# Two blocks of the second product in seven quarter products, with a new order table

## The chip, the cores and the metric

The kernel runs on one NeuronCore of one Trainium2 chip. The metric is the device time of one execution in microseconds; the figure before the change is the median of three runs. All times of single instructions come from one further, profiled execution.

## What is computed

Windowed attention with global tokens (8 batches, 8 heads, 512 local and 32 global tokens, head size 64) feeds a two-layer block with the gate h·cos(h). The second layer's product, `g @ w_out`, is what the change touches.

```python
s_ll = np.where(np.abs(pos[:, None] - pos[None, :]) <= 32, scale * q_l @ k_l.T, -1e9)
out_l = sm(concat([scale * q_l @ k_g.T, s_ll])) @ concat([v_g, v_l])
out_g = sm(scale * q_g @ concat([k_g, k_l]).T) @ concat([v_g, v_l])
x = concat([out_g, out_l])        # 8*544 tokens x 512
h = x @ w_in                      # w_in 512 x 2048
g = h * np.cos(h)
return g @ w_out                  # w_out 2048 x 512
```

## The kernel before

All matrix operands are kept as pairs of 16-bit floats, a high and a low part. A product of two such pairs is three matmuls: high by high, high by low, low by high.

**The chunks.** The tokens of the second stage are cut into 17 chunks of 256: chunks 0 to 15 hold the local tokens (two per batch, so chunk c belongs to batch c // 2), chunk 16 (`NC`) all 256 global ones. The 2048 columns of `w_in` are cut into 8 blocks of 256 (`NS`, index j), each of two tiles of 128.

**The first product** of a block is `m1_a(c, j)` (L1369): 2 tiles x 4 slices of the inner dimension x 3 = 24 matmuls with 256 moving columns, each with its own weight load, into one PSUM bank `ph` (three of these rotate). The gate follows: `m1_b` (ScalarE L1386, VectorE L1387) makes the argument `u`, `m1_c` the sine (ScalarE L715), `m1_d` the gated value `gf` (VectorE L1404), its high part `gh` (ScalarE L1408) and its low part `gl` (GpSimd L1409). Eleven places (`NG`) hold `gh` and `gl`; three hold `u`.

**The second product** of a block is `m2_a(c, j)` (L1423 to L1425): the moving operand is a row tile of `w_out` with 512 columns, the weights are 128x128 pieces of `gh` or `gl`. 2 token halves k x 2 tiles x 3 = 12 matmuls of 512 columns go into `po[0]` and `po[1]`, two PSUM banks of 128x512, where all 8 blocks of a chunk are summed. `m2_b` scales `po[0]` out of PSUM on ScalarE (L1438) and `po[1]` on VectorE (L1436); the very last bank is split between both (L1432, L1433). `m2_c` writes it out (L1445, L1453).

**Around it** attention of batches 2 to 7 is spread over chunks 2 to 13: scores (L1125, L1126), minimum and exponent (VectorE L1142, ScalarE L715), normalizing and splitting (GpSimd L1171, L1178, ScalarE L1176), transposes by DMA (L1183) and the product with the values (L1215). Sine and exponent share line 715 and need different tables on ScalarE; each change of kind is an ACT_TABLE_LOAD.

**What sets the order.** The program emits its work in numbered steps (one call such as `m1_a(4, 2)` is one step). `ORDER` holds a string for each engine and one for the DMA queue of SyncE: `599x24` means the next 24 instructions of step 599 on that engine, `23.4` means instruction 4 of step 23. Consecutive entries are tied, so every engine runs exactly in the order of its string and waits in that order.

Of the kernel before, what the change touches and what calls it, by code (L numbers as in the profile page):

```python
# [22 lines left out]
        18x4 22x4 23.4 23.0 23.5 23.1x2 23.6 23.3 23.7 27x4 29.4x4 29.0x2 33 33.2 33.1 33.3 29x2 28x8  # L23
        34x8 35 35.4 35.1x3 35.5x2 40.4 49 35 40.0x2 40.5 40.2 40.6x2 40.3 57 39x8 69x4 41x8 74 74.2
        74.1 74.3 108 108.2 64x24 67x24 72x24 91x24 108.1 108.3 106x24 125x24 109 109.4 109.1 109.5
        109.2 109.6 109.3 109.7 135x7 110x2 110.4 110.2x2 110.5x3 135 143x6 112x8 113x4 124 127x4 141x8
        113x4 143x2 135x16 149x3 149.4 149.3 149.5x3 143x16 150 150.4 150.1 150.5 150.2 150.6 150.3
        150.7 151x8 155 155.4 155.1x3 152x8 156x20 157x8 164x8 189x5 189.6x5 189.5 189.11 164x16 170x5
        176x24 208 208.6x2 208.1x2 208.8x2 208.3x2 171x20 195x4 187x24 208 208.10x2 196 196.2 196.1
        196.3 206x19 227x24 229.6 206x5 229 229.0x3 229.8 229.3x2 229.9x3 229.5 250.6x2 250.0x2 250.8x3  # L30
        250.2x4 250.11 204 209x4 274x4 274.6x3 274.4 274.9x2 274.5 274.11 210x2 210.3 210.2 288.6x3
        288.0x6 288.9x3 300x4 300.6x4 300.4 300.10x2 300.5 230 231x8 233 233.2 233.1 233.3 248x24 272x24
        234 234.2 234.1 234.3 303.6 303.0x3 303.7x3 303.3x3 303.10x2 230x35 311x12 251 252x4 313x4 313.6
        313.4 313.7x5 313.5 253x4 251x35 318x5 318.6x2 318.5 318.8x4 325x3 325.6x6 325.3x3 275x12 276x8
        286x24 275x24 349x5 329x2 329.6 329.2x4 329.7x5 289x2 290 349x2 289x2 294x60 333.6x2 333.0x4
        333.8x2 333.4x2 333.10x2 289x32 307x60 319 322 339 339.6 339.1x2 339.7x2 339.3 339.9 349x17
        369x11 379x4 369x4 326x4 330x4 379x17 335x4 340x4 339x2 339.4x2 379x3 369x9 355x4 356x8 357
        351x2 351.6 351.2x2 351.7x3 351.4x2 351.10x2 371x4 372x8 392x24 407x24 421x24 382x4 394x12 433x2
        433.6x2 433.2 433.8x2 433.3x3 433.10x2 395x4 450.6x5 450.0x6 450.11 409x3 410 409 465.6x2
        465.0x4 465.8x4 465.4x2 394x24 431x24 424x3 435x4 424 448x24 463x24 436 451x3 452x4 479 481  # L40
        481.6 481.1x2 481.7x3 481.3x2 481.10x2 481.5 496 496.6x4 496.1x3 496.10 496.4x2 479x14 467x4
        468x8 479x9 482x4 494x19 496.11 494x5 483x8 489x60 451x33 497x2 498 512x24 529x24 497x2 514.6x2
        514.0 514.8x3 514.1x5 514.11 499x4 500 515x12 516x4 531 531.6 531.1x2 531.7 531.3 531.8x2 531.4
        531.10x2 531.5 517x4 544x21 546x4 546.6x4 546.4x2 546.10x2 533x4 562x24 550x4 583x24 544x3 564x3
        564.6 564.3x2 564.7 564.5 564.8x4 515x24 565x2 585.6x3 585.0 585.9x3 585.1x5 565x2 566x8 567 598
        598.6 598.1 598.7x4 598.2x4 598.11 612 612.6x3 612.1x3 612.9x3 612.4x2 596 586x36 587x4 588x8
        596x23 600x4 610x24 630 630.6 630.1 630.7 630.2x3 630.8x3 628x14 613x36 614x4 618x60 628x10
        643x24 631x4 651x24 630 630.5 645.6x4 645.0 645.10 645.1 645.11 645.2x4 632 653.6x3 653.0x3
        653.9x2 653.3x3 653.11 668x2 668.6 668.2 668.7 668.3x3 668.8x4 666x24 646x4 655x4 687x24 703x24
        673x36 674x4 689x3 689.6x2 689.3x3 689.8x3 690x4 689 691x8 705.6 705.0x4 705.7x2 705.4x2 705.9x3  # L50
        716x24 692 730x24 706x4 718.6x3 718.0 718.9x2 718.1 718.11 718.2x4 747x24 707x8 711x60 764x11
        720x4 733x36 734x4 750 732.6x5 732.0x3 732.11 732.3x3 764x13 749.6x3 749.0x2 749.9 749.2 749.10
        749.3 749.11 749.4x2 751 752 766 766.6x3 766.1x2 766.9 766.3x3 751x3 766.10x2 767x4 776x4 772x12
        787x17 774x3 772x12 807x24 787x7 774.6x6 774.3x3 793x36 794x4 789x3 789.6x2 789.3x3 789.8x2
        823x23 810x4 823 811x8 812 789x2 826x4 827x8 831x60 836x24 850x20 809x2 809.6x2 809.2 809.8x3
        809.3x3 809.11 840x4 866x24 850x4 825x5 825.6x4 825.5 825.10x2 838.6 838.0x2 838.7x5 838.2x4 852
        852.6x2 853x6 854x4 881x24 889x10 904x5 852.1x5 852.8x4 853x30 868x12 869x4 870 883x12 884x4
        889x14 891x12 893x4 904x19 906x12 911x36 912x4 925x24 927x12 928x4 929x8 930 941x24 943x12 944x4
        945x8 949x60 954x24 956x12 958x4 968x24 970x12 971x36 972x4 985x24 987x12 988 989x4 990 1002x24
        1004x12 1005x4 1010x24 1012x12 1014x4 1025x24 1027x12 1031x36 1032x4 1045x24 1047x12 1048x4  # L60
        1049x8 1050 1061x24 1063x12 1064x4 1065x8 1069x60 1074x24 1076x12 1078x4 1088x24 1090x12 1091x36
        1092x4 1104x24 1106x12 1107x4 1108 1119x24 1121x12 1122x4 1127x24 1129x12 1131x4 1142x24 1144x12
        1149x36 1150x4 1163x24 1165x12 1166x4 1167x8 1168 1179x24 1181x12 1182x4 1183x8 1187x60 1192x24
        1194x12 1196x4 1206x24 1208x12 1209x36 1210x4 1223x24 1225x12 1226 1227x4 1228 1240x24 1242x12
        1243x4 1248x24 1250x12 1252x4 1263x24 1265x12 1269x36 1270x4 1283x24 1285x12 1286x4 1287x8 1288
        1299x24 1301x12 1302x4 1303x8 1307x60 1312x24 1314x12 1316x4 1326x24 1328x12 1329x36 1330x4
        1342x24 1344x12 1345x4 1346 1357x24 1359x12 1360x4 1365x24 1367x12 1369x4 1380x24 1382x12
        1387x36 1388x4 1401x24 1403x12 1404x4 1405x8 1406 1417x24 1419x12 1420x4 1421x8 1425x60 1430x24
        1432x12 1434x4 1444x24 1446x12 1447x36 1448x4 1461x24 1463x12 1464 1465x4 1466 1478x24 1480x12
        1481x4 1486x24 1488x12 1490x4 1501x24 1503x12 1507x36 1508x4 1521x24 1523x12 1524x4 1525x8 1526  # L70
        1537x24 1539x12 1540x4 1541x8 1545x60 1550x24 1552x12 1554x4 1564x24 1566x12 1567x36 1568x4
        1580x24 1582x12 1583x4 1584 1595x24 1597x12 1598x4 1603x24 1605x12 1607x4 1617x24 1619x12
        1623x36 1624x4 1636x24 1638x12 1639x4 1640x8 1649x24 1651x12 1652x4 1653x8 1657x60 1662x24
        1664x12 1665x4 1673x24 1675x12 1676x36 1677x4 1687x24 1689x12 1697x24 1699x12 1702x24 1704x12
        1712x24 1714x12 1718x36 1724x24 1726x12 1729x24 1731x12 1732x60 1737x24 1739x12 1742x24 1744x12
        1747x24 1749x12 1752x24 1754x12 1757x24 1759x12 1762x24 1764x12 1772x24 1774x12 1777x24 1779x12
        1783x24 1785x12 1788x24 1790x12 1793x24 1795x12 1798x24 1800x12 1803x24 1805x12 1808x24 1810x12
        1818x24 1820x12 1823x24 1825x12 1829x24 1831x12 1834x24 1836x12 1839x24 1841x12 1844x24 1846x12
        1849x24 1851x12 1854x24 1856x12 1864x24 1866x6 1869x24 1871x6 1874x6 1875x6 1876x6 1877x6 1878x6
        1883 1879x2 1883x4 1879x4 1883 1884x6 1885x6 1886x6 1887x6 1888x6 1889x6 1890x6  # L80
    """,
    "Activation": """
# [153 lines left out]
P = 128  # L236
# [1491 lines left out]
```

## Time and profile before

| what | value |
|---|---|
| median of three runs | 939.87 us (938.67 to 942.12) |
| profiled execution, whole | 944.08 us |
| profiled execution, span from the first to the last instruction | 942.3 us |
| TensorE busy | 94% of the span |
| ScalarE busy | 72% |
| VectorE busy | 62% |
| GpSimd busy | 53% |
| granted TensorE clock, mean | 0.984 |

Times in the rows are microseconds from the start of the span. PE is TensorE, PEld its weight loads, ACT ScalarE, DVE VectorE, POOL GpSimd, SP the queue that issues nearly all DMAs. The duration shown for a matmul holds the time until its result is out, and overlaps with the next one; the pace is the distance between starts.

### The profile page before, as it was taken

How to read it: one execution, taken by the hardware profiler on the slowest of the kernel's cores; microseconds unless marked ns; L12 is line 12 of the kernel's file. 1: busy time of each engine (PE TensorE's matmuls, PEld its weight loads, DVE VectorE, ACT ScalarE, POOL GpSimd, SP SyncE). 2: the span in 40 equal slices, each digit the busy share in tenths (PEclk: the TensorE clock that was granted, in tenths of full speed). 3: DMA queues.
4: the chain of work that ended last, by engine and by line, in shares of the span. 5: the costliest groups of instructions: out<-in, count | busy, mean ns of one | idle time of the engine just before them, and what ended most of it. 6: DMA issues, size and time to landing. Idle time of an engine off the chain costs nothing.

```text
span 942.3 us, 20875 instructions
## 1 busy us (share of the span) xinstructions
PE 886.3 (94%) x7892; PEld 611.9 (65%) x7892; DVE 585.8 (62%) x1536; ACT 677.5 (72%) x1331; POOL 495.3 (53%) x731
## 2 busy tenths in 40 slices
PE   5689988789999999999999999989999999999998
PEld 4468745466766776756767667657767766666673
DVE  5998885778765776776676667665765444223230
ACT  4789988779998878967876777767787774444441
POOL 3477889815766455466562546555656552121220
PEclk9779999999999999999999999999999999999999
DMA  9774615875667466476456655645554421000000
GB/s 339 274 235 169 213 23 125 156 192 105 149 146 137 128 120 132 108 158 121 104 127 141 135 99 124 163 85 134 92 109 85 93 42 42 1 23 13 12 24 23
DMA packets 162422, 110.79 MB, mean 118 GB/s; under 512 B 140176, under 2 KB 142608, under 8 KB 160400
## 3 DMA queue, kind: packets, MB, share of 16 engines
q1 hardware_dynamic: 162176, 109.31, 47.8%
q8 instruction: 62, 1.02, 0.4%
q14 instruction: 40, 0.33, 0.1%
q10 hardware_dynamic: 144, 0.13, 0.1%
HBM read 51.61 MB, written 8.91 MB: 64 GB/s over the span
## 4 chain that ended last, share of the span: by engine, by line
PE 48%; ACT 16%; DVE 12%; DMA 10%; POOL 5%; issue 4%; SPq 1%; DVEq 0%; POOLq 0%; ACTq 0%
PE ph L1369 21%; PE po L1425 7%; PE po L1423 7%; PE po L1424 7%; ACT t L715 3%; DMA qkr<-qk 3%; ACT u L715 2%; DMA vr<-v 2%; ACT L715 2%; DVE u L1387 2%; PE acc L1215 2%; DMA ptb<-plx 1%; DVE gf L1404 1%; ACT u L1386 1%; ACT gh L1408 1%
## 5 line engine op out<-in xcount | busy, mean ns | idle before, releaser
L1369 PE MATMUL ph<-xh,wi_h 128*128 128x256 f16 x1024 | 281.5, 275 | 8.5 <-DVE gf L1404 7.5
L1369 PE MATMUL ph<-xl,wi_h 128*128 128x256 f16 x1024 | 281.7, 275 | 0.0
L1369 PE MATMUL ph<-xh,wi_l 128*128 128x256 f16 x1024 | 281.4, 275 | 0.4 <-POOL wi_l L457 0.4
L1409 POOL TENSOR_TENSOR gl<-gf,gh 128x512 f16<-128x512 f32 x136 | 159.4, 1177 | 226.2 <-ACT gh L1408 222.0
L1369 PEld LDWEIGHTS <-wi_h 128*128 128x128 f16 x2176 | 212.0, 99 | 49.5 <-issue 12.1
L1424 PE MATMUL po<-wo_l,gh 128*128 128x512 f16 x544 | 203.9, 379 | 1.5 <-POOL wo_l L457 1.5
L1423 PE MATMUL po<-wo_h,gh 128*128 128x512 f16 x544 | 201.5, 379 | 3.2 <-DVE o L1436 2.3
L1425 PE MATMUL po<-wo_h,gl 128*128 128x512 f16 x544 | 201.5, 379 | 1.6 <-POOL gl L1409 1.6
L1387 DVE SCALAR_TENSOR_TENSOR u<-ph,ca,u 128x512 f32<-128x512 f32 x136 | 101.2, 745 | 114.9 <-ACT u L1386 114.6
L715 ACT ACTIVATE t<-t,mn 128x224 f32<-128x224 f32 (+1 forms) x256 | 118.2, 463 | 51.6 <-DVE mn L1142 35.9
L1171 POOL TENSOR_SCALAR t<-t,sm 128x224 f32<-128x224 f32 (+1 forms) x192 | 85.3, 462 | 127.4 <-DVE sm L1162 104.0
L715 ACT ACTIVATE u<-u,halfpi 128x512 f32<-128x512 f32 x136 | 97.1, 720 | 61.8 <-DVE u L1387 61.2
L1404 DVE SCALAR_TENSOR_TENSOR gf<-u,ph 128x512 f32<-128x512 f32 x136 | 92.8, 684 | 76.5 <-ACT u L715 65.6
L1386 ACT ACTIVATE u<-ph,quarter,ca 128x512 int32<-128x512 f32 x136 | 103.9, 767 | 46.4 <-PE ph L1369 46.1
L1178 POOL TENSOR_TENSOR plx<-t,plx 128x192 f16<-128x192 f32 (+1 forms) x192 | 120.9, 654 | 24.5 <-ACT plx L1176 24.0
L1369 PEld LDWEIGHTS <-wi_l 128*128 128x128 f16 x1088 | 107.4, 99 | 14.5 <-POOL wi_l L457 0.6
L1408 ACT CAST gh<-gf 128x512 f16<-128x512 f32 x136 | 82.6, 614 | 46.2 <-DVE gf L1404 46.1
L1425 PEld LDWEIGHTS <-gl 128*128 128x128 f16 x544 | 53.2, 98 | 67.1 <-POOL gl L1409 2.5
L1424 PEld LDWEIGHTS <-gh 128*128 128x128 f16 x544 | 53.2, 98 | 55.2 <-issue 4.2
L715 ACT ACT_TABLE_LOAD x67 | 86.0, 1283 | 2.6 <-DVE gmn L768 1.4
L1423 PEld LDWEIGHTS <-gh 128*128 128x128 f16 x544 | 52.9, 98 | 52.3 <-issue 2.3
L1142 DVE CUSTOM_DVE_ANT_0 t<-ps,msk,al 128x192 f32<-128x192 f32 (+1 forms) x192 | 76.5, 427 | 9.5 <-PE ps L1126 9.3
(239 smaller groups left out, 1223.5 us busy)
## 6 DMA issues: line engine op xcount, KB each, us to landing
qkr<-qk SPq DMA_DIRECT2D x24, 608.0 KB, 4.5
vr<-v SPq DMA_DIRECT2D x8, 1280.0 KB, 6.6
out<-o SPq DMA_DIRECT2D x33, 256.0 KB, 2.0
kh<-qa SPq DMA_DIRECT2D x48, 152.0 KB, 2.7
wo_h<-wo SPq DMA_DIRECT2D x8, 512.0 KB, 4.5
wo_l<-wo SPq DMA_DIRECT2D x8, 512.0 KB, 4.3
qa<-kl SPq DMA_DIRECT2D x24, 152.0 KB, 2.5
kl<-kl SPq DMA_DIRECT2D x24, 152.0 KB, 3.1
```

The lines of the kernel that those rows point to most:

```text
L715: ins = nc.scalar.activation(*a, **k).ins
L1171: nc.gpsimd.tensor_scalar(t[:, h], t[:, h], r[:, h : h + 1], 1.0, op0=ALU.mult, op1=ALU.mult)
L1178: nc.gpsimd.tensor_tensor(lo[:, h], t[:, h], hi[:, h], op=ALU.subtract)
L1369: nc.tensor.matmul(ph[:, a], w[:, kc, f], x[:, kc, q], start=first and ip == 0, stop=last and ip == 2, skip_group_check=True,)
L1386: nc.scalar.activation(u.bitcast(I32), ph, AF.Identity, bias=quarter, scale=a)
L1387: nc.vector.scalar_tensor_tensor(u, ph, a, u.bitcast(I32), op0=ALU.mult, op1=ALU.subtract)
L1404: nc.vector.scalar_tensor_tensor(gf, w, 0.5, st.pop(("ph", c, j)).rearrange("p a b -> p (a b)"), op0=ALU.mult, op1=ALU.mult,)
L1408: nc.scalar.copy(gh, gf)
L1409: ins = nc.gpsimd.tensor_tensor(gl, gf, gh, op=ALU.subtract).ins
L1423: nc.tensor.matmul(po[k], gh[:, q], wo_h[:, f], start=(f == 0), stop=False)
L1424: nc.tensor.matmul(po[k], gh[:, q], wo_l[:, f], start=False, stop=False)
L1425: nc.tensor.matmul(po[k], gl[:, q], wo_h[:, f], start=False, stop=(f == NJ - 1))
```

## The change

In chunks 4 to 16 (`CW` = 4) the blocks j = 0 and 1 (`QS` = 2) of the second product are done in Strassen's form with seven products (the variant with few sums). A block is a product of a 256x256 piece of activations with a 256x512 piece of `w_out`; both are seen as 2x2 quarters, and seven products of 128 tokens x 128 x 256 columns replace eight. Each is again three matmuls (`three`), now with 256 moving columns. What it takes:

- four sums of activation quarters per block on VectorE, in `m1_d`; three of the results (128x384) are split into high and low parts `yh`, `yl` on ScalarE and GpSimd, and the fourth replaces a quarter of `gf`. The place of `u` holds the sums until they are split;
- sums of weight quarters, once, in `w_sums`: at slots 25 and 27 of the schedule, and after chunk 3's last use of the plain weights;
- the results `c11`, `c12`, `c21`, `c22` are the four halves of the banks `po[0]` and `po[1]`. `sv_a` forms the first four products, `sv_y` the other three. Between them `sv_copy` moves the state of one half bank, scaled, into the output tile of another: three times per chunk from `c22` on ScalarE and once from `c12` on VectorE. At the end of a chunk `m2_b` adds `po` to that tile, now wholly on VectorE;
- the places for `gh` and `gl` are eight per chunk instead of eleven, since the sums need room;
- chunk 16 ends with its half k = 1 first and k = 0 last in the TensorE string; in the string of SP the output of k = 0 stands ahead of the output of k = 1;
- all five strings of `ORDER` are new, from the first step on, also for the steps that are as before.

```diff
         def m1_d(c, j):
             w = st.pop(("u", c, j))
-            s = (NS * c + j) % NG
+            s = (NS * (c - CW) + j) % (NG - QS - 1) if c >= CW else (NS * c + j) % NG
...
+            if seven(c, j):
+                a12, a11, a22, a21 = (gf[:, P * k : P * k + P] for k in range(4))
+                s2, s3, s4 = (w[:, P * k : P * k + P] for k in range(3))
+                nc.vector.tensor_tensor(s3, a11, a21, op=ALU.subtract)
+                nc.vector.tensor_tensor(a21, a21, a22, op=ALU.add)
+                nc.vector.tensor_tensor(s2, a21, a11, op=ALU.subtract)
+                nc.vector.tensor_tensor(s4, a12, s2, op=ALU.subtract)
...
+                sf = w[:, : 3 * P]
+                nc.scalar.copy(yh, sf)
+                nc.gpsimd.tensor_tensor(yl, sf, yh, op=ALU.subtract)
+        def three(o, g, w, start=False, stop=False):
+            (gh, gl), (wh, wl) = g, w
+            for n, (x, y) in enumerate(((gh, wh), (gh, wl), (gl, wh))):
+                nc.tensor.matmul(o, x, y, start=start and n == 0, stop=stop and n == 2, skip_group_check=True)
+        def sv_a(c, j):
...
+            c11, c12, c21, c22 = quarter_po(c)
+            three(c22, a11, wo_q(j, 0, 0), start=j == 0)
+            three(c12, s1, tw[j][0], start=j == 0)
+            three(c11, a12, wo_q(j, 1, 0))
+            three(c21, a22, tw[j][1])
+        def sv_copy(c, k, q):
+            o = st["ow", c][k // 2][:, k % 2 * HW : k % 2 * HW + HW]
+            if q == 3:
+                nc.scalar.activation(o, quarter_po(c)[q], AF.Identity, scale=st["co", c])
+            else:
+                nc.vector.tensor_scalar(o, quarter_po(c)[q], st["co", c], None, op0=ALU.mult)
+        def sv_y(c, j, k):
...
+            if k == 0:
+                three(c22, sk, tw[j][2])
+            elif k == 1:
+                three(c22, sk, wo_q(j, 0, 1))
+            else:
+                three(c12, sk, wo_q(j, 1, 1))
         def m2_b(c, k):
+            if c >= CW:
+                o = st["o", c, k] = st["ow", c][k]
+                for h in range(2 if c == NC else 1):
+                    x = slice(HW * h, HW * h + HW) if c == NC else slice(0, DM)
+                    nc.vector.scalar_tensor_tensor(o[:, x], po[:, x], sc, o[:, x], op0=ALU.mult, op1=ALU.add)
...
+                if c >= CW and j < QS:
+                    at(m + j // 2, m2, sv_a, c, j)
+                    for k in (0, 2, 1):
+                        at(m + (QS + 1) // 2, PI if k == 1 else m2, sv_y, c, j, k)
...
+                at(w - 1, ob, sv_copy, c, 0, 3)
+                at(w - 1, ob, sv_copy, c, 3, 1)
+                at(w, ob, sv_copy, c, 1, 3)
+                at(w, PJ, sv_copy, c, 2, 3)
```

## Rows read from the trace of the kernel before

**Rows 1.** The page, part 1: busy us, share of the span, instructions.

```profile
PE 886.3 (94%) x7892; PEld 611.9 (65%) x7892; DVE 585.8 (62%) x1536; ACT 677.5 (72%) x1331; POOL 495.3 (53%) x731
```

**Rows 2.** Busy time by stretch: stretch, length, PE, PEld, DVE, ACT, POOL, clock, DMA.

```profile
0.00:300.00 300.00, 258.81 (x2302) 181.91 (x2303) 229.64 (x639) 246.75 (x506) 200.28 (x311) 0.96 0.62 174
...
200.00:300.00 100.00, 95.41 (x889) 67.51 (x889) 75.37 (x222) 87.53 (x182) 61.31 (x96) 1.00 0.59 136
300.00:400.00 100.00, 97.01 (x1003) 70.27 (x1001) 70.99 (x188) 84.94 (x164) 50.95 (x79) 1.00 0.58 126
400.00:500.00 100.00, 97.82 (x909) 65.68 (x907) 67.46 (x181) 75.95 (x150) 60.48 (x88) 1.00 0.63 130
...
460.00:500.00 40.00, 40.00 (x378) 27.70 (x376) 29.48 (x81) 32.96 (x63) 27.12 (x40) 1.00 0.57 109
...
300.00:740.00 440.00, 429.78 (x4095) 299.70 (x4093) 293.58 (x787) 340.17 (x682) 238.07 (x353) 1.00 0.56 121
300.00:918.00 618.00, 607.78 (x5501) 421.13 (x5499) 354.23 (x895) 427.20 (x821) 292.76 (x419) 1.00 0.43 94
```

**Rows 3.** Timeline of ACT: the 33rd of L1386's 136, the first of chunk 4.

```profile
329.23 0.76 ACT L1386 ACTIVATE u<-ph,quarter,ca 128x512 int32<-128x512 f32 x1
```

**Rows 4.** Timeline of PE: first and last matmul of a first-product and a second-product block.

```profile
508.19 0.27 PE L1369 MATMUL ph<-xh,wi_h 128*128 128x256 f16 x1
...
510.70 0.27 PE L1369 MATMUL ph<-xh,wi_l 128*128 128x256 f16 x1
510.81 0.38 PE L1423 MATMUL po<-wo_h,gh 128*128 128x512 f16 x1
...
513.40 0.25 PE L1125 MATMUL ps<-kh,qa 128*128 128x192 f16 x1
```

**Rows 5.** Groups of instructions: line, engine, operation, shapes, count, busy us, mean ns, idle before.

```profile
L1387 DVE SCALAR_TENSOR_TENSOR u<-ph,ca,u 128x512 f32<-128x512 f32 x136 | 101.2, 745 | 114.9 <-ACT u L1386 114.6
L831 DVE TENSOR_REDUCE r<-pm_qk 128x2 f32<-128x128 f32 x24 | 6.8, 284 | 3.4 <-PE pm_qk L796 3.4
L787 DVE TENSOR_SCALAR qm<-qm 128x1 f32<-128x1 f32 x24 | 3.6, 149 | 0.3
L1438 ACT ACTIVATE o<-po,co 128x512 f32<-128x512 f32 x17 | 11.5, 678 | 9.3 <-PE po L1425 9.3
L1176 ACT CAST plx<-t 128x384 f16<-128x384 f32 x48 | 24.1, 502 | 1.2 <-POOL t L1171 1.2
L715 ACT ACT_TABLE_LOAD x67 | 86.0, 1283 | 2.6 <-DVE gmn L768 1.4
L1409 POOL TENSOR_TENSOR gl<-gf,gh 128x512 f16<-128x512 f32 x136 | 159.4, 1177 | 226.2 <-ACT gh L1408 222.0 <-PE ph L1369 4.1
L1178 POOL TENSOR_TENSOR plx<-t,plx 128x224 f16<-128x224 f32 x96 | 66.7, 714 | 8.3 <-ACT plx L1176 8.3
```

**Rows 6.** Timeline of the last six microseconds: PE, DVE, SP and ACT.

```profile
937.37 0.38 PE L1425 MATMUL po<-wo_h,gl 128*128 128x512 f16 x1
937.79 0.48 DVE L1432 TENSOR_SCALAR o<-po,co 128x256 f32<-128x256 f32 x1 [16.25 <-PE po L1425]
938.30 0.56 SPq L1453 DMA_DIRECT2D out<-o  x1
938.36 0.47 ACT L1433 ACTIVATE o<-po,co 128x256 f32<-128x256 f32 x1 [9.11 <-DVE o L1432]
938.86 0.66 ACTq L1453 DMA_DIRECT2D out<-o  x1
```

**Rows 7.** DMA issues of that stretch: KB each, median us to landing.

```profile
out<-o SPq DMA_DIRECT2D x1, 256.0 KB, 2.9
out<-o SPq DMA_DIRECT2D x1, 128.0 KB, 2.3
out<-o ACTq DMA_DIRECT2D x1, 128.0 KB, 2.4
```

**Rows 8.** Timeline of PE at the end of chunk 0: next matmul into an evacuated bank.

```profile
158.16 0.38 PE L1423 MATMUL po<-wo_h,gh 128*128 128x512 f16 x1 [1.63 <-DVE o L1436]
```

More of the change, by code (lines that the diff above doesn't have):

```diff
@@ L273 @@
 NG = 11
+CW = 4
+QS = 2
+TS0 = 25
 TWOPI = 6.283185
@@ L1365, in m1_a @@
             for a, kc in todo:
[L1366 removed]
+                f2 = 2 * j + (1 - a if seven(c, j) else a)
+                f = slice(f2 * P, (f2 + 1) * P)
                 first, last = (a, kc) == (0, 0), (a, kc) == (1, NPAIR - 1)
@@ new lines, in w_sums @@
+        def w_sums(j, late):
+            f0, f1 = 2 * j, 2 * j + 1
+            hi = slice(HW, DM)
+            r = [mp.tile([P, DM], F32, tag="o", name=f"ws{i}_{j}_{late}") for i in range(2)]
+            if late:
+                q = r[0].rearrange("p (a b) -> p a b", a=2)
+                nc.vector.tensor_tensor(q[:, 0], wo_h[:, f0, hi], wo_l[:, f0, hi], op=ALU.add)
+                nc.vector.tensor_tensor(q[:, 1], wo_h[:, f1, hi], wo_l[:, f1, hi], op=ALU.add)
+                nc.vector.tensor_tensor(q[:, 0], q[:, 1], q[:, 0], op=ALU.subtract)
+                nc.scalar.copy(wo_h[:, f0, hi], q[:, 0])
+                nc.gpsimd.tensor_tensor(wo_l[:, f0, hi], q[:, 0], wo_h[:, f0, hi], op=ALU.subtract)
+                return
+            for i, f in enumerate((f0, f1)):
+                nc.vector.tensor_tensor(r[i], wo_h[:, f], wo_l[:, f], op=ALU.add)
+            b11, b12, b21, b22 = r[0][:, :HW], r[0][:, hi], r[1][:, :HW], r[1][:, hi]
+            nc.vector.tensor_tensor(b11, b12, b11, op=ALU.subtract)
+            nc.vector.tensor_tensor(b22, b22, b11, op=ALU.subtract)
+            nc.vector.tensor_tensor(b21, b21, b22, op=ALU.subtract)
+            for i, t in enumerate((b11, b21, b22)):
+                h, l = tw[j][i]
+                nc.scalar.copy(h, t)
+                nc.gpsimd.tensor_tensor(l, t, h, op=ALU.subtract)
@@ new lines, in sv_out @@
+        def sv_out(c):
+            st["ow", c] = [mp.tile([P, DM], F32, tag="o", name=f"o_{c}_{k}") for k in range(2)]
+        def sv_copy(c, k, q):
[5 more added lines that the diff above has]
+        def sv_y(c, j, k):
+            y = st["y", c, j]
+            sk = tuple(t[:, P * k : P * k + P] for t in y)
+            c12, c22 = quarter_po(c)[1], quarter_po(c)[3]
+            if k == 0:
[4 more added lines that the diff above has]
+                three(c12, sk, wo_q(j, 1, 1))
@@ L1418, in m2_a @@
             po = st["po", c]
+            first = 0 if c < CW else -1
             for k in range(k0, k1):
```

503 lines of the change are left out of this document (294 added, 209 removed), and 22 rows, old and new, of the table ORDER.

## The prediction

> **What bounds the kernel now.** I read the busy shares first [rows 1]: TensorE is busy 94% of the span, no other engine over 72%. The stretches then show where that holds [rows 2]. In the first 300 us TensorE is busy 258.8 us, so about 41 us are waits of the opening, in which loads, weight decoding and the first batches decide. From 300 to 918 us it is busy 607.8 of 618 us: 10.2 us of waiting in two thirds of the run. Chunk 4, the first one changed, has the argument of its first block at 329 us [rows 3], so all that the change removes lies in the stretch where TensorE's own work sets the end. The granted clock there is 1.00 [rows 2], the level of 2.4 GHz, so the pace needs no correction.
>
> The pace is read from starts, not from the durations [rows 4]. 24 matmuls of 256 columns take 510.81 - 508.19 = 2.62 us, 0.109 us each, each with a weight load of its own. 12 matmuls of 512 columns take 513.40 - 510.81 = 2.59 us, 0.216 us each.
>
> **What TensorE is spared.** A plain block of the second product is 12 x 0.216 = 2.59 us. The new form has 7 x 3 = 21 matmuls of 256 columns. That is the shape of the first product (128x128 weights loaded each time, 256 columns moving), so I take its pace: 21 x 0.109 = 2.29 us. The block saves 0.30 us; 13 chunks x 2 blocks = 26 blocks save **7.7 us**. Doubling the short pace and comparing with the long one gives 2 x 0.109 - 0.216 = 0.002 us as the fixed part of a matmul, so nine more instructions per block cost nothing that matters.
>
> The Trainium skill speaks against this (TensorE: Matmul & The Clock Gate, section "Back-to-back issue gap"): it gives a sustained pace of about 81 ns at 128 columns and 131 ns at 512 when each matmul brings its weights. By an estimate on that line (about 98 ns at 256) the new block would take 2.06 us and the old 1.57, and the change would add 13 us. The trace disagrees: 216 ns at 512, not 131.
>
> **What the other engines get.** Per changed chunk:
> - VectorE: 8 sums of 128x128. The trace has no such sum; from below it is the 149 ns of an almost empty operation, the nearest row by size is a reduction over 128 columns at 284 ns, from above it is the 745 ns of 512 columns [rows 5]. I take 284: 2.3 us. One copy of a half bank, 0.48 us as in the last stretch [rows 6], and `m2_b` for both banks instead of one, +0.75 us. Together 3.5 us.
> - ScalarE: 2 casts of 128x384 at 502 ns and 3 half-bank copies at 0.47 us [rows 5, 6], less one evacuation of 678 ns: 1.7 us.
> - GpSimd: 2 subtractions of 128x384, between the rows for 224 and 512 columns (714 and 1177 ns), about 0.95 us each [rows 5]: 1.9 us.
>
> The ScalarE string brings more. I followed the string and counted where a step of the exponent kind gives way to one of the sine kind or back: 67 changes in the old string, which is the count of table loads in the row, and 77 in the new. Chunks 4 to 13 have 22 turns to the sine in the old and 28 in the new, so about 12 of the loads fall there: 12 x 1.28 = 15 us [rows 5].
>
> From 300 to 740 us ScalarE is busy 340.2 of 440 us, VectorE 293.6, GpSimd 238.1 [rows 2]. Nine to ten chunks add 16 + 15 us to ScalarE (77% becomes 84%), 33 to VectorE (67% becomes 74%), 18 to GpSimd (54% becomes 58%). None becomes the bound. Cover is another matter: ScalarE runs in order, and a late cast or argument makes TensorE wait. From above: the step from 400-500 to 300-400 us is one from 76% to 85% of ScalarE, and TensorE's share falls from 97.8 to 97.0%; 0.8% of 440 us is 3.5 us. From below: at 460-500 us ScalarE is at 82% and TensorE waits for nothing [rows 2]. I take **+0.5 us**, nearer to the lower end, since the new string places the sums' products eight to thirteen blocks behind their first product where the old had six; bounds 0 and 3.5. Below nothing is possible too, as the new string may also remove some of the 10.2 us of waits.
>
> The sums of the weights are made once, about 7 us of VectorE, 3 of ScalarE, 5 of GpSimd. They fall at 230 to 370 us, where TensorE has its 95 to 97%, and nobody waits for them before chunk 4's products. I cost them at nothing; without that cover it is at most the 7 us of VectorE, spread over two places.
>
> **Locks on a PSUM bank.** The new form reads half a bank while the products go on in the other half. The last stretch shows what that costs here [rows 6]: L1433 reads the right half of the bank whose left half L1432 reads, needs nothing of its result, and still starts 0.09 us after it has ended. So the bank, not the half, is handed from engine to engine. The Trainium skill (PSUM — Partial Sum Buffer, "PSUM bank collisions raise a hardware error") asks for that by bank and quadrant; if halves could be used apart, the sum would be 0.7 us lower.
>
> A copy that TensorE has to wait for costs: last matmul at 937.37 plus its slot of 0.22 is 937.59; the copy starts at 937.79, and the next user of the bank at 938.36: **0.77 us** per exposed copy. There are 4 copies x 13 chunks = 52. I followed the TensorE string and added, for each, the matmuls that stand between the last one into the bank ahead of the copy and the first one into it behind. In chunks 4 to 15 it is 0.8 to 15 us each time. Those are covered, if ScalarE and VectorE reach the copy at once. In chunk 16 two places have nothing between: `m2_b(15, 1)` on VectorE stands directly between the last product of chunk 15 and the first of chunk 16, both in `po[1]` (0.77 + 0.745 - 0.48 = 1.0 us; at the end of chunk 0 the same handover made TensorE wait 1.63 us [rows 8]), and the first copy of `c22` between `sv_a` and `sv_y` (0.77 us). The remaining two copies have 0.87 and 0.86 us of products as cover. Together **+1.8 us**, bounds 0.7 and 3.
>
> **The end.** Before, the two halves of the last bank leave one after the other, 0.48 + 0.47 us, and three output DMAs follow; the last lands 2.4 us after its issue. After it, two halves on VectorE take the same. But SP issues the whole row block of k = 0 (256 KB, 2.9 us to land) and only then its half of k = 1, since this stands behind it in the string, though ready since some 8 us: one more issue of 0.56 us ahead of 2.3 us [rows 6, 7]. 0.56 + 0.56 + 2.3 against 0.66 + 2.4 us: **+0.5 us**, bounds 0 and 1.
>
> **The sum.** -7.7 + 0.5 + 1.8 + 0.5 = -4.9 us. The profiled execution of 944.08 us would become 939.2. It is 4.2 us above the median of 939.87, and no term is tied to what that run had more of, so the median would become **935.0 us**.
>
> **The rivals.**
> - ScalarE decides. Its table loads and casts make the wait for arguments and low parts longer between 330 and 740 us. For it: 84% in order with loads of 1.28 us; against it: 460-500 us. The upper bound in place of the 0.5: **938 us**.
> - Banks lock TensorE out. If ScalarE comes to a copy late, behind an exponent group or a table load, TensorE waits at `sv_y` or `m2_a` although the string has cover. Each costs 0.77 us and with a table load ahead 2 us. Seven exposed copies of 52 eat the gain; from about 13 on the kernel is slower by over 0.5%. At 16, some with a load: **948 us**. For it: three of four copies are on the engine that fills most. Against it: the cover is mostly 2 to 8 us.
> - The opening. The strings are new from the first step on, and 41 us of waits stand there. In SP's string three of the eight loads of `w_in` now stand ahead of the last two query loads of batch 0. An opening 6 us shorter gives **929 us**, one 6 us longer 941 us; nothing in the trace of before decides this.
> - Short matmuls are not half as long as the long ones in the new place, and the 26 blocks save nothing: 942.7 us. The rows of the first product speak against it [rows 4]. The pace that the Trainium skill gives (same section as above) would lengthen the run in the same way, to about 953 us by the estimate, and falls by the same rows.
>
> **How the numbers follow.** Forecast 0.46; ScalarE 0.22; banks 0.14; opening shorter 0.10, longer 0.06; pace 0.02. A measurement can tell about 0.5% from no change, which is 4.7 us, so the forecast lies at the border. Its own spread (932 to 938) puts rather more than half of it below 935.2; with the shorter opening and a little of the ScalarE case, faster is 0.42. Slower than 944.6 takes most of the banks case, a third of the longer opening and the tail of the ScalarE case: 0.18. The rest, 0.40, is within 0.5%. The range reaches to the shorter opening below and into the banks case above: 929 to 946.
>
> **What would show it.** Right, if blocks of `sv_a` and `sv_y` run at 0.109 us a matmul, TensorE's busy time falls by 7 to 8 us, ACT_TABLE_LOAD counts 77, and TensorE's waits from 330 to 740 us stay near 10 us. Chunk 16 should show a wait of about 1.0 us for VectorE's evacuation and one of about 0.8 us for ScalarE's copy. Wrong, if waits for copies of half banks come up in many chunks, if casts of ScalarE head the list of TensorE's waits, or if chunk 4's first argument starts at another time than 329 us by more than 2 us: then the opening decides.

## The result

The changed kernel takes 927.9 us (median of 4 runs, 926.53 to 930.31), the kernel before on the same chip 940.4. The ratio is 0.987, with an interval of 0.984 to 0.990: 12.4 us less, where 4.9 were forecast. The time lies 1.1 us below the predicted range.

The profiled execution took 926.53 us, with a span of 924.7. Part 1 of its page, busy us by engine, answers to [rows 1]:

```profile
PE 876.5 (95%) x8126; PEld 634.2 (69%) x8126; DVE 633.4 (68%) x1684; ACT 707.6 (77%) x1400; POOL 511.3 (55%) x765
```

TensorE's busy time is 9.8 us less, and its idle time in the span fell too, from 56.0 to 48.2 us. Together that is 17.6 us, more than the 12.4 us between the medians: the profiled execution of the kernel before lies above its median, and this one is the shortest of its four, so differences between the two profiles overstate the gain by about 5 us. The busy times by stretch of the changed kernel (columns as in [rows 2]) show where:

```profile
0.00:300.00 300.00, 262.10 (x2333) 185.31 (x2334) 239.62 (x656) 251.95 (x516) 200.44 (x318) 0.96 0.63 177
200.00:300.00 100.00, 94.07 (x884) 66.66 (x883) 84.30 (x216) 87.83 (x179) 63.40 (x103) 1.00 0.61 137
...
300.00:740.00 440.00, 436.74 (x4352) 324.78 (x4350) 324.31 (x890) 376.34 (x743) 254.19 (x383) 1.00 0.55 119
300.00:918.00 618.00, 613.37 (x5791) 448.61 (x5790) 392.88 (x1027) 455.70 (x884) 310.88 (x447) 1.00 0.43 93
```

From 300 to 918 us TensorE waits 4.6 us, where it was 10.2 [rows 2]. In the first 300 us it waits 37.9 us, where it was 41.2. From 300 to 740 us alone it waits 3.3 us for 10.2. Only from 200 to 300 us did it lose: 94.1 us of work against 95.4, with VectorE at 84 against 75. TensorE's waits of the changed kernel from 300 us on (what waited, for what: us, times, longest):

```profile
PE acc L1274 <- DMA ptb<-plx: 2.0, 5, 0.6
PE po L1530 <- DVE o L1595: 1.2, 3, 0.8
PE po L1530 <- ACT o L1558: 0.6, 1, 0.6
PE po L1530 <- DVE o L1560: 0.5, 1, 0.5
PE ph L1432 <- DVE gf L1467: 0.3, 1, 0.3
```

From the same list for the kernel before:

```profile
PE pm_qk L796 <- DVE mn L1142: 3.1, 2, 2.5
PE acc L1215 <- DMA ptb<-plx: 3.1, 3, 1.4
...
PE po L1423 <- ACT o L1438: 0.7, 1, 0.7
PE po L1423 <- DVE o L1436: 0.7, 1, 0.7
```

The `po` lines are the banks: 2.3 us in all, 0.75 us of them in chunk 16 (0.19 and 0.56); before, 1.4 us. The rest, 2.3 us, is about a quarter of what stood there before. Three matmuls of the new form in a row, and the last six microseconds, answering to [rows 4] and [rows 6], from the timeline of the changed kernel (start, duration):

```profile
331.86 0.27 PE L1530 MATMUL po<-wo_h,gh 128*128 128x256 f16 x1
331.97 0.27 PE L1530 MATMUL po<-wo_l,gh 128*128 128x256 f16 x1
332.08 0.27 PE L1530 MATMUL po<-wo_h,gl 128*128 128x256 f16 x1
...
918.67 0.38 PE L1587 MATMUL po<-wo_h,gl 128*128 128x512 f16 x1
919.09 0.88 DVE L1595 SCALAR_TENSOR_TENSOR o<-po,co,o 128x256 f32<-128x256 f32 x2 [5.75 <-PE po L1587]
920.00 1.27 SPq L1622 DMA_DIRECT2D out<-o  x2
```

The pace is 0.11 us, as for the first product. From the start of the last matmul to the end of the span it is 6.0 us; it was 4.9.

The prediction named one more sign, the start of chunk 4's first argument, and [rows 3] put it at 329 us. That row is a later one: its instruction is the 38th of the 136, the sixth of chunk 4. The 33rd, the first of chunk 4, starts at 299.08 us in the kernel before and at 294.69 us in the changed one (timelines of ACT):

```profile
299.08 0.76 ACT L1386 ACTIVATE u<-ph,quarter,ca 128x512 int32<-128x512 f32 x1
294.69 0.77 ACT L1449 ACTIVATE u<-ph,quarter,ca 128x512 int32<-128x512 f32 x1
```

The second products of chunk 4 come behind it, so the stretch from 300 us on is still where all that the change removes lies. But the argument comes 4.4 us earlier, more than the 2 us beyond which the prediction said that the opening decides. In two further runs, described below, it comes 1.8 us earlier (the changed kernel once more) and 10.7 us earlier (the plain products in the new order).

### The profile page after: what moved, and what is told of

It reads as the page before. It is cut to its first block, busy times and chain, and to the rows that moved or that the text cites. A ratio compares the mean times of both kernels' runs of the same rounds, so it can differ in the third digit from the quotient of the medians.

```text
span 924.7 us, 21457 instructions
## 1 busy us (share of the span) xinstructions
PE 876.5 (95%) x8126; PEld 634.2 (69%) x8126; DVE 633.4 (68%) x1684; ACT 707.6 (77%) x1400; POOL 511.3 (55%) x765
## 4 chain that ended last, share of the span: by engine, by line
PE 56%; ACT 11%; DVE 11%; POOL 11%; DMA 5%; issue 4%; SPq 1%; DVEq 0%; POOLq 0%; ACTq 0%
PE ph L1432 23%; PE po L1587 7%; PE po L1585 7%; PE po L1586 7%; PE po L1530 4%; DMA ptb<-plx 3%; ACT t L774 2%; PE acc L1274 2%; ACT L774 2%; POOL t L1230 2%; POOL gl L1479 2%; POOL plx L1237 2%; DVE kl L917 1%; POOL plx L819 1%; ACT u L774 1%
## 5 line engine op out<-in xcount | busy, mean ns | idle before, releaser
L1586 PE MATMUL po<-wo_l,gh 128*128 128x512 f16 x440 | 161.9, 380 | 0.0
L1585 PE MATMUL po<-wo_h,gh 128*128 128x512 f16 x440 | 157.3, 381 | 0.7 <-DVE o L1605 0.7
L1587 PE MATMUL po<-wo_h,gl 128*128 128x512 f16 x440 | 157.9, 381 | 0.0
L1237 POOL TENSOR_TENSOR plx<-t,plx 128x192 f16<-128x192 f32 (+1 forms) x192 | 113.0, 612 | 32.8 <-ACT plx L1235 19.9
L774 ACT ACT_TABLE_LOAD x77 | 98.8, 1283 | 1.2
L1587 PEld LDWEIGHTS <-gl 128*128 128x128 f16 x440 | 43.1, 98 | 51.2 <-issue 0.7
L1586 PEld LDWEIGHTS <-gh 128*128 128x128 f16 x440 | 43.1, 98 | 46.8 <-issue 1.7
L1585 PEld LDWEIGHTS <-gh 128*128 128x128 f16 x440 | 42.8, 98 | 42.6 <-issue 1.5
```

The costliest lines, as they stand in the source:

```text
L774: ins = nc.scalar.activation(*a, **k).ins
L1237: nc.gpsimd.tensor_tensor(lo[:, h], t[:, h], hi[:, h], op=ALU.subtract)
L1585: nc.tensor.matmul(po[k], gh[:, q], wo_h[:, f], start=(f == first), stop=False, skip_group_check=c >= CW)
L1586: nc.tensor.matmul(po[k], gh[:, q], wo_l[:, f], start=False, stop=False, skip_group_check=c >= CW)
L1587: nc.tensor.matmul(po[k], gl[:, q], wo_h[:, f], start=False, stop=(f == NJ - 1), skip_group_check=c >= CW)
```

## The experiments

The numbers of each run are the median, then the ratio to the kernel before with its 95% interval.

### The order and the form apart

The plain products in the new order, from the first step to the last:

```diff
 TensorE's string, chunks 4 to 16
-sv_a(c, 0) x12 ... sv_y(c, 0, 0) x3 ...
+m2_a(c, 0) x12 ...
-w_sums, sums and casts of m1_d, sv_copy    (all engines)
```

Two things of the changed kernel stay in this run beside the order: from chunk 4 on there are eight places for `gh` and `gl` instead of eleven, and VectorE does all evacuations of the output banks.

> The plain products of the kernel before in the new order from start to end: where the new table has the seven-product matmuls of a block, the twelve plain ones stand; the weight sums, the activation sums and their casts and the early copies are gone, and the evacuations of chunks 4 to 16 are all VectorE's, as in the kernel after. Theory A: the idle time of TensorE falls as in the kernel after (3.3 us in the first 300 us and about 5 us later), so 932 to 934 us, a ratio near 0.992; then the form itself is worth only the rest, 928 less 933 = -5 to -6 us. Theory B: 939 to 941 us, a ratio of 0.999 to 1.001, and the form is worth the whole 12 us. Halfway, at 936 to 937, both have a share.

Beside it, the opening's order alone, in the old string:

```diff
 every string: the steps of slots 0 to 21
-in the old relative order
+in the new relative order, at the same positions
```

> The kernel before, with one thing changed: the instructions of the opening (the steps planned into the first 22 slots) stand on every engine in the relative order that the new table gives them; no product has the seven-product form, and the rest of the order is the old one. Theory A (the surplus over the eight microseconds of removed products comes from the new order): the TensorE idle time of the first 300 us falls by the 3.3 us that the two traces differ by, so about 937 us against 940.4, a ratio of 0.996. Theory B (the surplus comes from the form itself, because a lighter TensorE is less often the one that is waited for): no change, 940 us, a ratio of 0.999 to 1.003.

And the changed kernel once more on that chip:

> The changed kernel as it is, beside the others on one chip, so that the differences to it are read without a change of chip. Both theories: 928 us, a ratio of 0.987.

Measured: the plain products in the new order 928.2 us, 0.9865 [0.9845, 0.9885]; the changed kernel 927.9 us, 0.9862 [0.9845, 0.9880]; the opening alone 944.6 us, 1.0041 [1.0018, 1.0064].

So the order without the form gives the whole 12 to 13 us, more than theory A had, and the seven products, as they stand in the changed kernel, give nothing on top. The opening alone is no gain but a loss, which neither of its theories had. Part 1 of the page of the plain products in the new order:

```profile
PE 882.0 (95%) x7892; PEld 610.5 (66%) x7892; DVE 584.1 (63%) x1551; ACT 679.2 (73%) x1327; POOL 483.8 (52%) x731
```

And its busy times by stretch:

```profile
0.00:300.00 300.00, 264.87 (x2463) 189.82 (x2464) 233.16 (x657) 255.47 (x527) 199.61 (x314) 0.97 0.65 180
200.00:300.00 100.00, 98.77 (x1010) 71.67 (x1009) 75.03 (x216) 90.85 (x187) 61.86 (x99) 1.00 0.66 146
300.00:918.00 618.00, 613.54 (x5415) 419.26 (x5414) 350.06 (x893) 423.69 (x801) 284.23 (x418) 1.00 0.42 91
```

The waits fall by 6.1 us in the first 300 us (35.1 for 41.2) and by 5.7 us after them (4.5 for 10.2): 11.8 us, nearly the whole gain. The evacuations and the places begin with chunk 4, so they can hardly have shortened the first 300 us; after them the waits for a bank were 1.4 us before, and what the eight places do was not tested apart.

The two traces also differ in TensorE's busy time, 882.0 for 886.3 us with the same 7892 matmuls, at a mean granted clock of 0.987 for 0.984. That is not a gain of the order: 13 executions of the kernel before on this chip had 0.985 to 0.990, the four of this run 0.981 to 0.987, and in three more runs of the new order (the fillers below) the same matmuls were busy 880.7 to 888.0 us.

Against this run the changed kernel waits as little from 300 us on, with fewer matmul microseconds to do. It loses from 200 to 300 us, where TensorE has 94.1 us of work against 98.8 here.

### Where the form's gain goes

The weight sums left out:

```diff
-three(c12, s1, tw[j][0], start=j == 0)      -three(c21, a22, tw[j][1])     -three(c22, sk, tw[j][2])
+three(c12, s1, wo_q(j, 0, 1), start=j == 0) +three(c21, a22, wo_q(j, 1, 1)) +three(c22, sk, wo_q(j, 1, 0))
-at(TS0 + 2 * j, PJ, w_sums, j, 0)           -at(slot0(CW - 1) + LAG + 3 + j, PJ, w_sums, j, 1)
```

> The changed kernel without its weight sums: the 16 additions and subtractions on VectorE, the 8 casts on ScalarE and the 8 subtractions on GpSimd are left out, and the seven products read stored quarters of the weight in place of the sums (so this computes something else, with the same matmuls of the same shapes). Theory E (in the new order the form gains its 7.7 us of TensorE and gives most of them back between 200 and 300 us, where the weight sums make VectorE late: the idle time of TensorE there is 6.4 us against 1.2 in the run of the plain products): idle there back to 1 to 2 us, the one VectorE step of 6.54 us (the low half of a key tile) back to under 2.5 us, and 920.5 to 923 us, a ratio of 0.979 to 0.981. Rival F (the form's gain is eaten by the chunks themselves, by activation sums, casts and handed-over banks): 926 to 928 us.

Measured: 917.0 us, 0.9744 [0.9722, 0.9766], by the ratios 11 us less than the changed kernel. Theory E holds, and more came back than its 5 to 7 us. The stretch from 200 to 300 us of this run:

```profile
200.00:300.00 100.00, 99.52 (x1013) 71.99 (x1012) 75.85 (x220) 91.78 (x185) 63.01 (x101) 1.00 0.66 147
```

In the changed kernel, one instruction stands out there. It makes the low half of a key tile from two tensors of SBUF (`kl`), and takes 1.48 us at its median. VectorE's timeline, and GpSimd's from 240 us on (start, duration):

```profile
249.67 6.54 DVE L917 SCALAR_TENSOR_TENSOR kl<-qkr,qs,qa 128x1216 f16<-128x1216 f32 x1
...
240.44 2.13 POOL L1230 TENSOR_SCALAR t<-t,sm 128x224 f32<-128x224 f32 x5 [3.59 <-DVE sm L1221]
242.54 0.67 POOL L1513 TENSOR_TENSOR twgh<-ws,twgh 128x256 f16<-128x256 f32 x1
243.18 0.82 POOL L1230 TENSOR_SCALAR t<-t,sm 128x192 f32<-128x192 f32 x2
...
248.26 1.68 POOL L1237 TENSOR_TENSOR plx<-t,plx 128x224 f16<-128x224 f32 x3
249.90 0.67 POOL L1513 TENSOR_TENSOR twwfo<-ws,twwfo 128x256 f16<-128x256 f32 x1
...
252.66 2.26 POOL L1479 TENSOR_TENSOR gl<-gf,gh 128x512 f16<-128x512 f32 x2
```

GpSimd works from 240.44 to 254.92 us without a pause; the step ends at 256.21, 1.29 us behind it. TensorE pays for it a few microseconds later. Its waits from 200 to 300 us in the second run of the changed kernel:

```profile
PE ps L1185 <- DMA kl<-kl: 3.3, 1, 3.3
PE pm_v L855 <- DVE vm L486: 2.3, 1, 2.3
```

Both stand behind the step: `kl` is what it makes, `vm` is the next instruction of VectorE's string.

Two of GpSimd's subtractions for the weight sums were moved ahead, to break its run:

```diff
 GpSimd's string
 w_sums(1, 0): twgl
+w_sums(1, 0): twgh, twwfo
 ...
-w_sums(1, 0): twgh
 ...
-w_sums(1, 0): twwfo
```

> The changed kernel with two GpSimd instructions elsewhere: the last two subtractions of the weight sums, which start at 243.1 and 250.4 us, stand directly behind the one at 227.0 us, so that GpSimd's unbroken run of work around the VectorE step of 6.54 us (250.2 to 256.8 us) begins earlier and has a gap in it. Theory G (VectorE's step does not get on while GpSimd works without a gap, and TensorE's 6.4 us of idle time after it come from that step): the step takes 1.5 to 3 us, the idle time of 200 to 300 us falls by 3 to 5 us, 923 to 925.5 us. Rival H (VectorE is late by the sum of all its added work there, 8 us, whatever that one step takes): the step gets shorter but the time stays at 927 to 929 us.

Measured: 927.2 us, 0.9844 [0.9825, 0.9862], no gain. But not as rival H has it: the step at 250 us became short, and the one before it long. VectorE and GpSimd of this run:

```profile
225.88 8.67 DVE L1001 SCALAR_TENSOR_TENSOR kl<-qkr,qs,qa 128x1216 f16<-128x1216 f32 x1
...
231.59 1.69 POOL L1321 TENSOR_TENSOR plx<-t,plx 128x224 f16<-128x224 f32 x3
```

GpSimd's run ends at 233.28, the step 1.27 us later. The collision was moved, not removed. So all three were set where GpSimd has nothing to do:

```diff
 GpSimd's string
-w_sums(1, 0): twgl   ...  twgh   ...  twwfo
 ...
 m1_d(3, 1)
+w_sums(1, 0): twgl, twgh, twwfo
```

> The changed kernel with three GpSimd instructions later: the subtractions of the second block's weight sums, which started at 227.0, 243.1 and 250.4 us, stand at the place where GpSimd runs dry (255.5 us in the changed kernel, idle there for 6.8 us); nothing needs them before 333 us. Theory G (a VectorE step on two float tensors of SBUF waits for a gap in GpSimd's work and then takes its 1.3 us; the run that moved two of these instructions ahead only moved the collision, to 8.67 us at 225.9 us, where GpSimd worked from 222.0 to 233.3 us without a gap and the step ended 1.3 us behind it): with the run broken the step at 250 us takes under 3 us, no other of these steps takes over 3 us, the idle time of TensorE between 200 and 300 us falls from 6.4 to 1 to 3 us, and the time to 920 to 924 us. Rival H (VectorE is late by the 8 us of its own additions, whatever the step takes): the step is short and the time stays at 926 to 928 us.

Measured: 920.7 us, 0.9756 [0.9731, 0.9782]. No `kl` step takes over 2.5 us, TensorE is busy 99.1 us from 200 to 300 us. Theory G's time came out. VectorE does all its additions as before (84 us busy there), so rival H is out.

### Which instruction

Each of these moves only some of the three to that place (`twgl` started at 227, `twgh` at 243, `twwfo` at 250 us).

> The changed kernel with one GpSimd instruction moved instead of three: only the subtraction that starts at 250.4 us, just behind the start of VectorE's step of 6.54 us, goes to the place where GpSimd runs dry; the ones at 227.0 and 243.1 us stay. Theory K (that one instruction, entered between two products of the attention, is what keeps the step out): the step at 250 us takes 1.5 to 1.7 us, TensorE's idle time from 200 to 300 us is 0.5 to 2 us, 920.5 to 923 us, ratio 0.976 to 0.979. Rival L (what counts is how late GpSimd is by all three): the step stays over 4 us and the time over 925 us.

> The other half: the two subtractions that start at 227.0 and 243.1 us go to the place where GpSimd runs dry, and the one at 250.4 us stays between the same two products. Theory K: the step still meets it and takes 5 to 7 us, 926 to 929 us, ratio 0.984 to 0.988. Rival L: the step under 3 us and 920 to 923 us.

> The changed kernel with only the subtraction that starts at 227.0 us moved to where GpSimd runs dry; the ones at 243.1 and 250.4 us stay. Theory P (the one at 243.1 us keeps the step out: it stands inside the unbroken run of GpSimd from 241 us on): the step at 250 us still takes 6.5 us, 924 to 928 us, ratio 0.983 to 0.987. Theory Q (the one at 227.0 us, through the earlier VectorE step beside it, which took 2.42 us in place of 1.79): the step under 2 us, 920 to 922 us, ratio 0.977 to 0.980.

> The changed kernel with only the subtraction that starts at 243.1 us moved to where GpSimd runs dry; the ones at 227.0 and 250.4 us stay. Theory P: the step at 250 us under 2 us, the subtraction behind its start held for 1.2 us instead, 920 to 922 us, ratio 0.977 to 0.980. Theory Q: the step still 6.5 us, 924 to 928 us.

| moved | step at 250 us | us | ratio |
|---|---|---|---|
| none (second run) | 6.54 | 927.9 | 0.9862 [0.9845, 0.9880] |
| `twwfo` | 6.56 | 925.3 | 0.9835 [0.9822, 0.9849] |
| `twgl` | 7.17 | 926.1 | 0.9842 [0.9823, 0.9862] |
| `twgh` | 1.57 | 920.9 | 0.9785 [0.9765, 0.9804] |
| `twgl`, `twgh` | 1.56 | 921.0 | 0.9783 [0.9770, 0.9796] |
| all three | 1.57 | 920.7 | 0.9756 [0.9731, 0.9782] |

Theory K falls with the first of these runs. L came out in the first two and falls, with Q, by the last two: `twgl` and `twgh` are equally long and both stand ahead of the step, and only `twgh` matters. P holds: the single subtraction of 0.67 us at 243 us decides. With it moved, VectorE's step gets in 0.25 us after its start, and it is GpSimd's next instruction that is held. VectorE and GpSimd in the run with `twgh` moved:

```profile
244.67 0.42 POOL L1314 TENSOR_SCALAR t<-t,sm 128x192 f32<-128x192 f32 x1
245.13 0.61 POOL L1321 TENSOR_TENSOR plx<-t,plx 128x224 f16<-128x224 f32 x1
...
249.84 1.57 DVE L1001 SCALAR_TENSOR_TENSOR kl<-qkr,qs,qa 128x1216 f16<-128x1216 f32 x1
...
250.09 1.85 POOL L1597 TENSOR_TENSOR twwfo<-ws,twwfo 128x256 f16<-128x256 f32 x1
```

1.85 us in place of 0.67. The first two lines show one more difference to the changed kernel: GpSimd pauses here from 245.09 to 245.13 us, and there its run has no pause from 240.44 us on. In the run with `twgl` moved the step lost, and the moved instruction made GpSimd's run longer, and the step with it:

```profile
249.03 7.17 DVE L1001 SCALAR_TENSOR_TENSOR kl<-qkr,qs,qa 128x1216 f16<-128x1216 f32 x1
...
254.24 0.68 POOL L1597 TENSOR_TENSOR twgl<-ws,twgl 128x256 f16<-128x256 f32 x1
```

Again the step ends (256.20) 1.28 us behind GpSimd's run (254.92).

### Making the collision on purpose

In the plain products in the new order, where no such step is late, GpSimd got instructions on scratch tiles: three of them ahead of its row of four products, then one inside the row, then one inside the row with the operand types of the weight sums.

```diff
+nc.gpsimd.tensor_tensor(t[:, :256], t[:, 256:512], t[:, 512:768], op=ALU.subtract)   # x3, or x1
+nc.gpsimd.tensor_tensor(t[:, 256:512], r[:, :256], t[:, :256], op=ALU.subtract)      # r float32
```

> The plain products in the new order (the run that had no weight sums and no late VectorE step, 928.2 us, ratio 0.9865), with one thing added: three subtractions of 128x256 on GpSimd, on a scratch tile that nothing reads, placed ahead of the run of GpSimd work around 245 to 253 us (and one fill of that tile earlier). Nothing waits for them, VectorE, ScalarE and TensorE have no instruction more. Theory G (VectorE's step on two SBUF tensors waits for a gap in GpSimd's work): GpSimd, 2 us later, no longer waits for ScalarE between its products, the step at 247.3 us (1.56 us) ends 1.3 us behind GpSimd's run, at about 256 us, so 5 to 9 us long, TensorE's idle time from 200 to 300 us goes from 1.2 to 4 to 7 us, and the time to 933 to 938 us, ratio 0.992 to 0.997. Rival H (the loss in the changed kernel came from VectorE's own 8 us of additions): 928 to 929 us, ratio 0.985 to 0.988.

> The plain products in the new order with one GpSimd subtraction of 128x256 added on a scratch tile (and one fill of that tile earlier), now exactly where one of the weight sums' subtractions stands in the changed kernel: between the third and the fourth product of the row of four at 245.9 us. In the run before, three such subtractions stood 1.6 us ahead of that row, and VectorE's step still got in between the third and the fourth product (the fourth took 1.74 us in place of 0.56 us while the step ran), as in the plain run without a filler. Theory G, narrowed (the step can begin only where GpSimd pauses, that boundary is such a pause, and an instruction set into it takes the pause away): the step at 247 us lasts until 1.3 us behind the end of GpSimd's run at 253.8 us, so about 7.5 us, TensorE's idle time between 200 and 300 us goes from 1.2 to 4 to 7 us, and the time to 932 to 937 us, ratio 0.990 to 0.996. Rival (any boundary will do, and the changed kernel's 6.54 us had another cause): the step stays under 3 us and the time at 928 to 930 us.

> The plain products in the new order with one GpSimd subtraction on scratch tiles between the third and the fourth product of the row at 245.9 us, as in the run with a filler of two float16 inputs there, but with the types of the weight sums' subtraction (float32 less float16, float16 out). In that run the filler itself was held for 1.2 us and VectorE's step got in. Theory M (the types decide who is let in): the step lasts to 1.3 us behind GpSimd's run, 5 to 9 us, and 932 to 937 us, ratio 0.990 to 0.996. Rival N (they do not): the step under 2 us, the filler held for about 1.2 us, ratio 0.984 to 0.988.

Measured: 930.1 us, 0.9887 [0.9863, 0.9911]; 926.2 us, 0.9855 [0.9837, 0.9873]; 925.8 us, 0.9843 [0.9830, 0.9856]. The plain run had 0.9865. The step took 1.57, 1.56 and 1.57 us; each time it got in at once. The filler inside the row was the one that was held:

```profile
251.17 1.56 DVE L967 SCALAR_TENSOR_TENSOR kl<-qkr,qs,qa 128x1216 f16<-128x1216 f32 x1
...
251.40 1.86 POOL L1525 TENSOR_TENSOR filler<-filler 128x256 f16<-128x256 f16 x1
```

So the collision could not be made to order: neither an instruction at the place nor its types is enough. Theory G as I narrowed it (only a pause right there lets the step in) falls; M falls too. Whether an unbroken run is enough, these three runs do not show, for in each of them GpSimd still paused for 0.03 to 0.08 us, 3 to 5 us ahead of the step. In all traces of the new order, the step at 250 us lost where no such pause was left (six traces) and got in where there was one. That does not make the pause the cause: in the run with `twgh` and `twwfo` moved ahead, the step at 225.88 us lost although GpSimd had been idle for 1.3 us until 222.04 us. What stays: once the step has lost, it ends 1.27 to 1.29 us behind the end of GpSimd's run, in all eight traces with a long step. What makes it lose is open.

### The cover of the early copies

```diff
 TensorE's string, chunks 7, 10, 11, 13, 14, 15
+m1_a and attention matmuls
 sv_a(c, 0), sv_a(c, 1)
-m1_a and attention matmuls
 sv_y(c, 0, 0)
```

> The changed kernel with one thing changed: in six of the twelve middle chunks (7, 10, 11, 13, 14, 15) the matmuls that stand between the four seven-product sums into the output banks and the first product that must wait for the early copy are moved ahead of those sums, so that the copy (0.4 us on VectorE, 0.5 us on ScalarE) has nothing beside it. Theory C (a copy of half a bank holds TensorE for its own length and the hand-over, 0.8 us, when it is not covered, as the copies of chunk 16 do): plus 6 times 0.6 to 0.9 us, so 931.5 to 933.5 us, and six waits on the early copies in TensorE's waits. Rival D (TensorE makes the time good later, since it waits elsewhere for ScalarE): within 1 us of the changed kernel.

Measured: 951.6 us, 1.0125 [1.0101, 1.0148], 24 us more than with the cover. TensorE's waits from 300 us on, first lines:

```profile
PE ph L1515 <- DVE gf L1550: 9.6, 5, 2.5
PE acc L1357 <- DMA ptb<-plx: 3.8, 3, 3.0
PE po L1613 <- ACT o L1641: 2.5, 5, 0.6
PE po L1613 <- DVE o L1643: 1.9, 2, 1.3
```

The waits for a bank are now 5.6 us (with 1.2 us in a third line that is not shown), 3.3 more than with the cover: 0.55 us for each of six chunks, just under the price that theory C put at 0.6 to 0.9. But that is a seventh of the loss. The moved matmuls now come before their buffers are free (9.6 us for `gf`), and TensorE's busy time grew from 877.4 to 886.6 us at a mean granted clock of 0.975 in place of 0.986. D falls; C has the right wait and the wrong total.

### The end

```diff
 SyncE:   -m2_c(16, 0), m2_c(16, 1)
          +m2_c(16, 1), m2_c(16, 0)
 TensorE: -m1_a(16, 7) x24 ... sv_a(16, 1) x12, sv_y(16, 0, 0) x3, sv_y(16, 1, 0) x3
          +sv_a(16, 1) x12, m1_a(16, 7) x12, sv_y(16, 0, 0) x3, sv_y(16, 1, 0) x3, m1_a(16, 7) x12
 ScalarE, VectorE: the gate of that block, m1_b to m1_d(16, 7), behind the early copies
```

> The changed kernel with two things changed at the end: SyncE's queue issues the half output that is ready first (of the rows whose sums end first) ahead of the whole one that waits for the last product, and the last block of the first product is moved, in two halves, between the seven-product sums of chunk 16, so that they cover the early copies. Theory: 0.6 us from the queue (its second issue now waits 0.63 us behind the first) and the 0.75 us of waits in chunk 16, so 1.0 to 1.4 us less, 926.5 to 927 us. Rival: the work that follows the moved block comes late for the last sums, and TensorE waits there instead: 928 us or more.

> Both edits of the two runs before it together: by theory G and the theory of the end 922 to 924.5 us; by rival H 926.5 to 928 us.

> The same three GpSimd instructions later, with the two edits at the end (the queue's order and the last block between the sums of chunk 16), which alone gave about 2 us of the changed kernel: by theory G 918.5 to 922.5 us, by rival H 924 to 926 us.

Measured: 925.6 us, 0.9825 [0.9807, 0.9843]; with the moved-ahead subtractions 927.3 us, 0.9835 [0.9817, 0.9854]; with the three later ones 920.3 us, 0.9757 [0.9732, 0.9782]. From the start of the last matmul to the end of the span it is 5.2 us (918.06 to 923.3) in place of 6.0. Over its three pairs the edit moves the ratio by -0.4, -0.1 and 0.0%: the 1.0 to 1.4 us forecast are no more than these runs can tell. The three subtractions placed later, with or without the end, are faster than both kernels: by 7 to 10 us than the changed one, by 22 us than the one before.

## Why the prediction was wrong, step by step

- **What TensorE is spared: right.** The pace of the new form is 0.11 us. In the new order the form is worth 0.8 to 1.1% once the late step is gone (0.9865 against 0.9785 and 0.9756, give or take 0.3%), 7.5 to 10 us; the sum had -7.7 for the products and 2.8 of costs. The Trainium skill's pace (TensorE: Matmul & The Clock Gate, "Back-to-back issue gap"), by which the form would lose, falls by the same run.
- **What the other engines get: right.** From 300 to 740 us ScalarE is busy 376.3 us, VectorE 324.3 and GpSimd 254.2, where the additions made 371, 327 and 256.
- **The order: the step that failed.** I allowed that the new string "may also remove some of the 10.2 us of waits" and took +0.5 us, from ScalarE's fill alone. The waits fell to 4.6 us, and without the form to 4.5, and those of the opening by 6.1 us in the plain run. Where the sum had +0.5 us for waits, the plain run has 11.8 us fewer. I had put the opening at nothing, since nothing in the trace of before decides it. Its own signs said so: the waits that were to stay near 10 us did not, and chunk 4's first argument came earlier, by 10.7 us in the plain run. The rival with the shorter opening, 929 us, came nearest, but that is luck, for it is not its mechanism: the opening's steps alone made the kernel 0.4% slower, so the gain needs the order behind them too, and half of it lies behind 300 us. Which part of that order earns it was not separated.
- **"The pace needs no correction": right**, at a granted clock of 1.00 from 300 to 918 us in both traces.
- **The weight sums "at nothing", at most 7 us: wrong in kind.** They cost 11 us with everything, and 7 to 10 of these come back with three of GpSimd's subtractions elsewhere, so most of it is not their length. One subtraction of 0.67 us kept one step of VectorE waiting for 5 us, and TensorE behind it. My bound added up the work; it did not ask whom the work meets. No row of before has a `kl` step of over 2.1 us, so this could not be read off, but that the step and GpSimd's work run side by side could.
- **Banks: right in place, too large.** In chunk 16 the two waits that I named are there, 0.19 and 0.56 us for 1.0 and 0.77. Three more of 1.5 us together stand in other chunks. Against the 1.4 us of before that is +0.9 us in all, for +1.8. Cover that hides a copy is real, as taking it away showed.
- **The end: +1.1 us for +0.5**, just over the upper bound. The numbers set beside that term add up to 0.36 and not to 0.5. The queue's order that I named has most of it: with that order turned, 0.8 us come back.
- **Table loads: right.** The groups of instructions of the changed kernel have 77:

```profile
L774 ACT ACT_TABLE_LOAD x77 | 98.8, 1283 | 1.2
```

They decided nothing. "ScalarE decides" and "banks lock TensorE out" did not come.

Put together, by the ratios: the order gives 12.7 us less, the form 7.5 to 10 us less, the collision takes 7 to 10 us back. I missed the first and the third, which are of opposite sign, and had the form 3 to 5 us too small. That the result is only 7.5 us off the forecast is owed to misses that partly cancel.

## What to carry to other kernels

When a change brings a new order with it, run the old work in the new order first: here that showed that what looked like the gain of an algorithm was that of a schedule, and that the algorithm's own gain was being lost. Cost side work not by its length but by what it runs beside: list the steps of the late engine whose duration is far from their median, and see what its neighbour did at that time. Here one such piece of 0.67 us, moved to where the neighbour is idle, gave 7 us; moved ahead with another, it only met an earlier step.

## What the runs showed of the hardware

The VectorE step `kl`, which has two SBUF inputs, and GpSimd's work keep each other out. If the step at 250 us gets in, it takes 1.56 us for 1.48 and GpSimd's instruction is held for 1.2 us (1.85 for 0.67). If not, it waits for the whole of GpSimd's unbroken run and ends 1.27 to 1.29 us behind it, 6.5 to 8.7 us long. The Trainium skill names the two engines' shared SBUF interfaces (GPSIMD Engine Reference, "Specifications"), with contention for VectorE instructions that have two SBUF inputs. The trace agrees, and the step that lost is 5 to 7 us longer for it.
